# A three-stage fp32 kernel: wider blocks at the end of its first MLP, and Pool's work cut into pieces

## The chip, the cores and the metric

The kernel runs on one core of one Trainium2 chip, in one launch. The metric is device time in microseconds (us). The core has a matrix engine (PE, with its weight loads shown apart as PEld), a vector engine (DVE), a scalar engine (ACT), GpSimd (called POOL in the profile, Pool here) and a queue (SP) that issues the DMA transfers. Each engine works through its own list of instructions in the order in which they were written down; engines wait for each other by semaphores.

## The reference

Three stages, all in fp32, each fed by the one before:

```python
# attention: q, k, v are (4, 8, 576, 64); everything below max - tau is masked
scores = q @ k.T / sqrt(64)
scores = where(scores >= max(scores) - tau, scores, -1e9)
x = softmax(scores) @ v                  # then (2304 tokens, 512)
# first MLP: 512 -> 2048 -> 512
h = x @ w_in;  y = (h / (1 + exp(-h))) @ w_out
# second MLP: 512 -> 1536 -> 512
out = ((y @ w_a) * (y @ w_b)) @ w_o2
```

## The kernel before, in words

**Products.** A product in fp32 is made of passes in a faster format: each operand is cut into a high and a low part (`hi`, `lo` in the code: hi is a rounded copy made by ACT, lo is the difference) and three passes are summed in PSUM (weights low, weights high, other operand low). A pass loads 128x128 weights and streams the other operand's columns: 256 columns in the first MLP (`TB = 256`, nine blocks of tokens), 512 in the second (`T2 = 512`).

**Weights.** They come from HBM as pairs of 32-bit words. One chunk (128x512) goes through `split_weight`: ACT copies the low word (L314), ACT or DVE scales the high one (L319/L321, tile `wc`, one buffer), DVE takes its sign (L325, in place in `wraw`) and joins both (L330), Pool adds the words (`total`, L334, tile `wt`), ACT rounds (`hi`, L338), and Pool or DVE subtracts (`lo`, L342). The first MLP has 32 chunks, prepared during attention, all with `lo` on Pool; the second has 36, alternately on Pool and DVE.

**Attention.** A tile is 128 queries by 576 keys. PE makes the scores (L483, later L476), DVE scales them and takes the minimum (L492), adds tau (`thr`, L498 in the first 16 tiles, L500 behind them), ACT takes the exponential (L504/L506), DVE masks and sums (L509), PE transposes (L541; L539 are filler transposes), ACT copies out of PSUM (L548), PE multiplies by v (L586). Pool divides by the sums (L621) and, in the later heads, makes a low part of q (L407; k's on DVE, L404). The result x goes to DRAM.

**First MLP.** Block j of 256 tokens: x is read back and cut (`xr`; hi on ACT L676, lo on Pool L679). For each of 16 slices f of the hidden size: 12 passes up (L704, PSUM bank `hb` or `hc`), tanh on ACT (L713), gate on DVE (L716), hi on ACT (L719), lo on DVE (L722), 12 passes down (L754, PSUM pair `sb` or `sd`). The passes of later blocks lie between attention's.

**Second MLP.** Up passes L833 into `ps_a` and `ps_b`, L840 to L849 for the product and its parts, down passes L877.

**What sets the order.** Every operation is a task of a `Plan` with an engine, a cost in ns, a rank and the tasks it needs. `Plan.run` plays them through with these costs and writes each engine's list in the order of its play. Tasks marked `port` are DVE's that use the SBUF port that DVE has together with Pool; the plan makes such a task, and any Pool task, longer by what the other has still to run, at most by its own cost (`SHARED = 1.0`). `closed` is the point where attention's buffers are given back and those of the later stages opened; `closed1` is the same behind the first MLP.

Of the kernel before, what the change touches and what calls it, by code (L numbers as in the profile page):

```python
# [21 lines left out]
P = 128  # L22
# [10 lines left out]
NB = NT // TB  # L33
# [25 lines left out]

SCALE_ON = ("ACT",)  # L60


class Plan:
# [15 lines left out]

    SHARED = 1.0  # L80
# [42 lines left out]
    def run(self):  # L123
# [17 lines left out]
        while events:  # L141
# [13 lines left out]
            for e, q in ready.items():  # L155
                if idle[e] and q:
# [50 lines left out]
def fused_kernel(ctx: ExitStack, tc: tile.TileContext, qk, qk2, v, tau, w_in, w_out, w_a, w_b, w_o2, out):  # L207
# [19 lines left out]
    def pool(stack, name, bufs, side="left", **kw):  # L227
# [22 lines left out]
    ps_1 = pool(p1, "ps_1", 1, space=PSUM)  # L250
    ap = {n: pool(att, n, RINGS[n]) for n in ("qk", "v", "t", "e", "pa", "pb")}
# [36 lines left out]

    def dma(rank, nbytes, fn, n=1, **kw):

        return pl.add("SP", 400 * n, rank, fn, nbytes=nbytes, **kw)
# [8 lines left out]
    def split_weight(key, src, rank, dst, after=(), lo_engine="Pool", scale_engine="DVE"):  # L300
# [32 lines left out]
        def total():  # L333
            nc.gpsimd.tensor_tensor(out=s["t"], in0=s["c"].bitcast(U32), in1=s["t"], op=ALU.add)  # L334
# [5 lines left out]
        def lo():  # L340
            eng = nc.gpsimd if lo_engine == "Pool" else nc.vector
            eng.tensor_tensor(out=wt[key][:, 1, :], in0=s["t"].bitcast(F32), in1=wt[key][:, 0, :].bitcast(F32),  # L342
                              op=ALU.subtract)
# [10 lines left out]
        i = pl.add("ACT", act_ns(512), rank, hi, [t], [dst], behind=after)  # L354
        o = pl.add(lo_engine, pool_ns(512) if lo_engine == "Pool" else dve_ns(512), rank, lo, [i], port=True)
        pl.free("wt", o)
        w_ready[key] = (i, o)
        return [a, l, c, h, j, t, i, o]
# [33 lines left out]
    def split_head(n, b, h):  # L392
# [13 lines left out]
        def lo_q():  # L406
            nc.gpsimd.tensor_tensor(out=s["t"][D:, 0], in0=s["r"][D:, :S], in1=s["t"][D:, 0].bitcast(F32), op=ALU.subtract)  # L407
# [3 lines left out]
        q = add("Pool", pool_ns(S), n + R_SPLIT, lo_q, [up])  # L411
        k = add("DVE", dve_ns(S), n + R_SPLIT, lo_k, [up], port=True)
        att_tasks.append(ld)
        pl.free("qk", q, k)
        s["ready"] = [q, k]
# [42 lines left out]
    def softmax(parts, total):  # L458
# [10 lines left out]
        def scores():  # L469
            s["s"] = (ps_1 if bank == "sb" else ps_s).tile([P, 2, 512], F32, name=bank)  # L470
# [24 lines left out]
        def threshold():  # L495
            s["thr"] = sm_p.tile([P, 1], F32, name="thr")
            if early:
                nc.vector.tensor_scalar(out=s["thr"], in0=s["min"], scalar1=back, scalar2=tsub, op0=ALU.mult, op1=ALU.add)  # L498
            else:
                nc.vector.tensor_add(out=s["thr"], in0=s["min"], in1=tadd)  # L500
# [27 lines left out]
    def weigh(b, half, c, tiles, v, last):  # L528
# [91 lines left out]
        def divide():  # L620
            nc.gpsimd.tensor_tensor(out=s["x"][:, :nq], in0=s["x"][:, :nq], in1=s["i"][:, :nq], op=ALU.mult)  # L621
# [9 lines left out]
        dv = add("Pool", pool_ns(nq), last_n + R_EV, divide, [ld])  # L631
        pl.free("xi", dv)
        st2 = dma(-1, P * 4 * nq, store, after=[dv])
        pl.free("x", st2)
        att_tasks.extend([st, ld, st2])
# [54 lines left out]
    def mlp1_up(n, j, f):  # L690
# [34 lines left out]
        for c in range(NC):  # L725
            p = pl.add("PE", 3 * pe_ns(TB), R, up(c),
# [4 lines left out]
            if f == NF - 1:  # L731
                pl.free("xb", p)
        th = pl.add("ACT", act_ns(TB, True), R_AUX, tanh, [p], ["g", "th"])
        ga = pl.add("DVE", dve_ns(TB), R_AUX, gate, [th])
        pl.free(bank, ga)
        hh = pl.add("ACT", act_ns(TB), R_AUX, hi, [ga])
        ll = pl.add("DVE", dve_ns(TB), R_AUX, lo, [hh], port=True)
        pl.free("th", ll)
        g_ready[j, f] = (hh, ll)

    def mlp1_down(n, j, f):


        ring = "sd" if j * NF >= TWO_H and j % 2 == 0 else "sb"
        prods = [(e, a, "gh") for e in range(NC) for a in (1, 0)] + [(e, 0, "gl") for e in range(NC)]

        def down(k0):
            def fn():
                if f == 0 and k0 == 0:
                    ys[j] = (pools["hc"] if ring == "sd" else ps_1).tile([P, 2, 512], F32, name=ring).rearrange("p k (e t) -> p (k e) t", e=2)  # L750
                w = wt["out", f]
                for e, a, g in prods[k0:k0 + 4]:

                    nc.tensor.matmul(ys[j][:, e, :], lhsT=w[:, a, e * P:(e + 1) * P], rhs=gs[j, f][g],  # L754
                                     start=(f == 0 and e % 2 == 0 and a == 1), stop=(f == NF - 1 and g == "gl"),
# [4 lines left out]
        for k0 in (0, 4, 8):  # L760
            p = pl.add("PE", 4 * pe_ns(TB), R, down(k0), [g_ready[j, f][k0 == 8], *w_ready["out", f]],
                       [ring] if f == 0 and k0 == 0 else [], behind=[down_last[0]])
            down_last[0] = p
        w_last["out", f] = p
        pl.free("g", p)
        if f == NF - 1:
            def halve(k):
                def fn():
                    ys[j, k] = yo_p.tile([P, 2, TB], F32, name="yo")
                    if k == 0:  # L770
                        nc.scalar.activation(out=ys[j, k], in_=ys[j][:, 2 * k:2 * k + 2], func=AF.Copy, scale=0.5)
                    else:
                        nc.vector.tensor_scalar(out=ys[j, k], in0=ys[j][:, 2 * k:2 * k + 2], scalar1=0.5, scalar2=None, op0=ALU.mult)
# [232 lines left out]
```

## Time and profile before

| | |
|---|---|
| runs | 1191.71 us, median of 3 (1190.04 to 1193.56) |
| profiled execution | 1190.77 us; its span in the trace 1189.0 us |
| PE busy | 1154.5 us (97%), 7675 passes |
| PE weight loads busy | 994.4 us (84%) |
| DVE busy | 646.2 us (54%) |
| ACT busy | 543.9 us (46%) |
| POOL busy | 255.2 us (21%) |
| granted TensorE clock | 1.00 of full speed (2.4 GHz) |

Shares over the whole span hide the stages. The page cuts the span into 40 slices of 29.7 us; a digit is the busy share of a slice in tenths. PE shows 7, 8 and 9 in the first seven slices and 9 nearly everywhere behind them; DVE shows 7 to 9 in the first seven, then 7 and 8 while attention lasts (to slice 16), little in the rest of the first MLP, 5 to 7 in four or five slices round its end, and 1 to 3 behind them; POOL is busy in the first seven slices and round the end of the first MLP. PE's ends are modelled, so its busy time says little between 95 and 100%; the times from start to start of its passes say more.

### The profile page before, as it was taken

Reading aid. Unit: us, or ns where it says so; the run is one execution under the profiler, and the core shown is the slowest. Engines: PE = TensorE matmul, PEld = TensorE weight load, DVE = VectorE, ACT = ScalarE, POOL = GpSimd, SP = SyncE. Lnnn points to the kernel's source line nnn. Section 1 sums busy time; section 2 is a strip of 40 time slices with the busy share of each in tenths; the row PEclk is TensorE's granted clock in tenths of the full one; section 3 lists DMA queues with packets and bytes.
Section 4 is the critical chain, followed back from the end, with each engine's and each line's share of the span. In section 5 each row is a group of like instructions: output and inputs, shape, how many; then the busy total and the mean of one; then the engine's idle time right before and its main releaser. Section 6 shows DMA issues by size and latency. Waiting matters only on the chain.

```text
span 1189.0 us, 19705 instructions
## 1 busy us (share of the span) xinstructions
PE 1154.5 (97%) x7675; PEld 994.4 (84%) x7675; DVE 646.2 (54%) x1448; ACT 543.9 (46%) x1071; POOL 255.2 (21%) x212
## 2 busy tenths in 40 slices
PE   8879999999999999989999999999999999999998
PEld 6556667898898888989999999877888888888898
DVE  7989897777777877473233257775211311211121
ACT  7777786666666766553233245443211211211121
POOL 3655554222111311131000034553000000000000
PEclk9999999999999999999999999999999999999999
DMA  5654543222322320261010024441100200000010
GB/s 192 197 175 144 168 155 132 77 85 81 100 74 71 108 73 33 67 191 54 1 37 28 1 72 143 127 139 56 69 1 1 71 1 1 18 36 1 1 36 18
DMA packets 43277, 90.15 MB, mean 76 GB/s; under 512 B 4384, under 2 KB 22448, under 8 KB 43184
## 3 DMA queue, kind: packets, MB, share of 16 engines
q1 hardware_dynamic: 43040, 88.89, 23.5%
q8 instruction: 60, 0.98, 0.3%
q14 instruction: 33, 0.27, 0.1%
q10 hardware_dynamic: 144, 0.00, 0.0%
HBM read 74.65 MB, written 14.23 MB: 75 GB/s over the span
## 4 chain that ended last, share of the span: by engine, by line
PE 65%; DVE 5%; DMA 3%; POOL 2%; issue 2%; ACT 1%; SPq 0%; POOLq 0%; DVEq 0%; ACTq 0%
PE op L877 11%; PE ps_b L833 11%; PE ps_a L833 10%; PE hb L704 8%; PE sb L754 7%; PE sd L754 4%; PE hc L704 4%; PE av L586 3%; PE sa L476 3%; PE tp L541 3%; POOL wt L334 2%; DVE wc L330 1%; DMA wraw<-w_a 1%; DVE wraw L325 1%; DVE wc L321 1%
## 5 line engine op out<-in xcount | busy, mean ns | idle before, releaser
L704 PE MATMUL hb<-xh,w 128*128 128x256 f32 x832 | 164.3, 291 | 3.1 <-DVE th L716 1.4
L843 DVE TENSOR_TENSOR z<-ps_b,z 128x512 f32<-128x512 f32 (+1 forms) x60 | 38.2, 637 | 230.8 <-PE ps_b L833 230.8
L833 PE MATMUL ps_a<-yh,w 128*128 128x512 f32 (+1 forms) x480 | 137.1, 370 | 0.3 <-POOL w L342 0.3
L833 PE MATMUL ps_b<-yh,w 128*128 128x512 f32 (+1 forms) x480 | 136.7, 369 | 0.4 <-DVE w L342 0.4
L704 PEld LDWEIGHTS hb<-xh,w 128*128 128x128 f32 x832 | 128.9, 191 | 9.1 <-issue 4.3
L877 PE MATMUL op<-w,zh 128*128 128x512 f32 x432 | 134.3, 392 | 0.0
L492 DVE TENSOR_SCALAR_CACHE_REDUCE t<-sa,nscale 128x576 f32<-128x576 f32 x128 | 103.5, 808 | 48.9 <-PE sa L476 47.6
L509 DVE SCALAR_TENSOR_TENSOR e<-t,thr,e 128x576 f32<-128x576 f32 x128 | 114.1, 891 | 16.7 <-ACT e L506 15.3
L704 PE MATMUL hb<-xl,w 128*128 128x256 f32 x416 | 117.5, 283 | 0.0
L334 POOL TENSOR_TENSOR wt<-wc,wt 128x512 uint32<-128x512 uint32 x68 | 91.9, 1351 | 114.2 <-DVE wc L330 93.4
L754 PE MATMUL sb<-gh,w 128*128 128x256 f32 x768 | 115.9, 286 | 0.0
L541 PE MATMUL tp<-ident,e 128*128 128x128 f32 x706 | 104.7, 277 | 10.6 <-DVE e L509 7.4
L506 ACT ACTIVATE e<-t,min 128x576 f32<-128x576 f32 x128 | 99.8, 782 | 25.4 <-DVE t L492 24.7
L840 ACT COPY z<-ps_a 128x512 f32<-128x512 f32 (+1 forms) x60 | 32.6, 543 | 163.1 <-PE ps_a L833 163.1
L541 PEld LDWEIGHTS tp<-ident,e 128*128 128x128 f32 x706 | 78.8, 140 | 32.4 <-DVE e L509 12.3
L754 PEld LDWEIGHTS sb<-gh,w 128*128 128x128 f32 x768 | 101.1, 191 | 3.3 <-issue 2.8
L833 PEld LDWEIGHTS ps_a<-yh,w 128*128 128x128 f32 x480 | 87.4, 188 | 17.3 <-POOL w L342 0.7
L833 PEld LDWEIGHTS ps_b<-yh,w 128*128 128x128 f32 x480 | 86.7, 188 | 16.2 <-DVE w L342 0.9
L877 PEld LDWEIGHTS op<-w,zh 128*128 128x128 f32 x432 | 80.3, 188 | 16.9
L846 ACT CAST zh<-z 128x512 fp32r<-128x512 f32 (+1 forms) x60 | 34.6, 577 | 128.3 <-DVE z L843 128.3
L722 DVE TENSOR_TENSOR gl<-th,gh 128x256 fp32r<-128x256 f32 x144 | 72.7, 505 | 33.9 <-ACT gh L719 33.6
L833 PE MATMUL ps_a<-yl,w 128*128 128x512 f32 (+1 forms) x240 | 88.9, 370 | 0.0
(97 smaller groups left out, 2173.3 us busy)
## 6 DMA issues: line engine op xcount, KB each, us to landing
qk<-qk SPq DMA_DIRECT2D x20, 576.0 KB
wraw<-w_in SPq DMA_DIRECT2D x16, 512.0 KB
wraw<-w_out SPq DMA_DIRECT2D x16, 512.0 KB
v<-v SPq DMA_DIRECT2D x20, 320.0 KB
wraw<-w_a SPq DMA_DIRECT2D x12, 512.0 KB
wraw<-w_b SPq DMA_DIRECT2D x12, 512.0 KB
wraw<-w_o SPq DMA_DIRECT2D x12, 512.0 KB
xr<-xT_d SPq DMA_DIRECT2D x36, 128.0 KB
```

Source lines behind the costliest of these rows:

```text
L334: nc.gpsimd.tensor_tensor(out=s["t"], in0=s["c"].bitcast(U32), in1=s["t"], op=ALU.add)
L476: nc.tensor.matmul(s["s"][:r + m, j, :NH], lhsT=hd["t"][:, 0, c - r:c + m], rhs=hd["t"][:, k, j * NH:(j + 1) * NH], start=(k == 1), stop=( ...
L492: nc.vector.tensor_scalar(out=s["t"], in0=s["s"][:, :, :NH], scalar1=nscale, scalar2=None, op0=ALU.mult, op1=ALU.min, accum_out=s["min"])
L506: nc.scalar.activation(out=s["e"], in_=s["t"], func=AF.Exp, scale=-1.0, bias=s["min"])
L509: nc.vector.scalar_tensor_tensor(out=s["e"], in0=s["s"][:, :, :NH] if early else s["t"], scalar=s["thr"], in1=s["e"], op0=ALU.is_ge if ear ...
L541: nc.tensor.transpose(t["tp"][:, j * P:(j + 1) * P], e["e"][:, o:o + P], ident)
L704: nc.tensor.matmul(s["h"], lhsT=w[:, a, o:o + P], rhs=xx, start=(c == 0 and k == 0), stop=(c == NC - 1 and k == 2))
L722: nc.vector.tensor_sub(out=s["gl"], in0=s["t"], in1=s["gh"].bitcast(F32))
L754: nc.tensor.matmul(ys[j][:, e, :], lhsT=w[:, a, e * P:(e + 1) * P], rhs=gs[j, f][g], start=(f == 0 and e % 2 == 0 and a == 1), stop=(f == ...
L833: nc.tensor.matmul(s[nm][:, :tn], lhsT=w[:, a, o:o + P], rhs=yy[:, :tn], start=(c == 0 and k == 0), stop=(c == NC - 1 and k == 2))
L843: nc.vector.tensor_mul(out=s["z"][:, :tn], in0=s["b"][:, :tn], in1=s["z"][:, :tn])
L877: nc.tensor.matmul(o_ps[t0, i], lhsT=s[z][:, i * P:(i + 1) * P], rhs=wt["o2", f][:, a, :], start=(f == 0 and k == 0), stop=(f == NF2 - 1 a ...
```

## The change

Two blocks of 512 tokens stand at the end of the first MLP in place of four of 256. They have buffers of their own (pool `b5`, open from `closed` on), an own PSUM bank for each of their output parts (`yc`, `yd`, `ye`, `yf`, or `sb`), and their loads of x stand behind `closed`. In the weights of the first MLP, `lo` moves from Pool to DVE. Pool's operations outside the second MLP's weights are cut into pieces of at most 128 columns. In attention's `thr`, L500 becomes a `tensor_scalar` with one per-partition operand where it was a `tensor_add`, and L498 takes a constant in place of one of its two. The plan lengthens a shared task by all that the other engine has still to run. The buffers of the second MLP's input are split in two (four for even blocks, four behind `closed1` for odd ones), its first four weight chunks go to the ring `w`, which comes free in the last block of the first MLP, and its last four to `w2`, which now opens at `closed1`.

```diff
-NB = NT // TB
+BLOCKS = tuple((i * TB, TB) for i in range(5)) + ((5 * TB, 512), (5 * TB + 512, 512))
+PIECE = 128
+LO_ON = ("DVE",)
...
-                        shared = max(0, min(port["Pool" if e == "DVE" else "DVE"] - now, t["cost"]))
-                        port[e] = end = done = end + self.SHARED * shared
+                        port[e] = end = done = end + max(0, port["Pool" if e == "DVE" else "DVE"] - now)
...
+def pieces(n, most):
+    k = -(-n // most)
+    return [slice(n * i // k, n * (i + 1) // k) for i in range(k)]
...
+    def on_pool(n, rank, fn, after, most):
+        ts = []
+        for o in pieces(n, most):
+            ts.append(pl.add("Pool", pool_ns(o.stop - o.start), rank, lambda o=o: fn(o), after, behind=ts[-1:]))
+        return ts
...
-        t = pl.add("Pool", pool_ns(512), rank, total, [j, l])
-        pl.free("wc", t)
+        ts = on_pool(512, rank, total, [j, l], most)
+        pl.free("wc", ts[-1])
...
-        engines = dict(scale_engine=SCALE_ON[i % len(SCALE_ON)])
+        engines = dict(scale_engine=SCALE_ON[i % len(SCALE_ON)], lo_engine=LO_ON[i % len(LO_ON)], most=PIECE)
...
-                nc.vector.tensor_add(out=s["thr"], in0=s["min"], in1=tadd)
+                nc.vector.tensor_scalar(out=s["thr"], in0=s["min"], scalar1=tadd, scalar2=None, op0=ALU.add)
...
-            ld = dma(-1, P * 4 * TB, load, after=need, take=["xr"], slack=SLACK)
-            h = pl.add("ACT", act_ns(TB), R_AUX, hi, [ld], ["xb"])
-            l = pl.add("Pool", pool_ns(TB), R_AUX, lo, [h])
-            pl.free("xr", l)
+            ld = dma(-1, P * 4 * tn, load, after=need, take=[raw], slack=SLACK, behind=[closed] if big else [])
+            h = pl.add("ACT", act_ns(tn), R_AUX, hi, [ld], [ring])
+            l = on_pool(tn, R_AUX, lo, [h], PIECE)[-1]
+            pl.free(raw, l)
...
-        ring = "sd" if j * NF >= TWO_H and j % 2 == 0 else "sb"
+        banks = {4: ("yc", "yd"), 5: ("ye", "yf", "sb"), 6: ("yc", "yd", "ye", "yf")}.get(j, ("sb",))
+        per = T2 // tn
...
-        split_weight(key, src, 1e6 + i, "w2" if i < RINGS["w2"] else "w", [closed], ("Pool", "DVE")[i % 2])
+        split_weight(key, src, 1e6 + i, *(("w", [closed]) if i < 32 else ("w2", [closed1])), ("Pool", "DVE")[i % 2])
```

How the lists change is read from the built programs. First DVE in the tiles behind the sixteenth, before the change; `t` and `e` are a tile's scores and exponentials, `wraw` and `wc` a weight chunk:

```order
L492 TENSOR_SCALAR t,min<-sa,nscale 128x576
L500 TENSOR_TENSOR thr<-min,tadd 128x1
L492 TENSOR_SCALAR t,min<-sa,nscale 128x576
L509 SCALAR_TENSOR_TENSOR e,sum<-t,thr,e 128x576
L325 TENSOR_SCALAR wraw<-wraw 128x512
L500 TENSOR_TENSOR thr<-min,tadd 128x1
L330 SCALAR_TENSOR_TENSOR wc<-wc,wraw 128x512
```

The same place now (L511, L519, L528 are the lines of scores, `thr` and mask; L341 and L346 of sign and join; L358 of `lo`):

```order
L358 TENSOR_TENSOR w<-wt,w 128x512
L341 TENSOR_SCALAR wraw<-wraw 128x512
L511 TENSOR_SCALAR t,min<-sa,nscale 128x576
L346 SCALAR_TENSOR_TENSOR wc<-wc,wraw 128x512
L519 TENSOR_SCALAR thr<-min,tadd 128x1
L528 SCALAR_TENSOR_TENSOR e,sum<-t,thr,e 128x576
```

Each chunk brings one more instruction on DVE, `lo` (L358), right ahead of the next chunk's sign. Pool in the same stretch, before:

```order
L342 TENSOR_TENSOR w<-wt,w 128x512
L334 TENSOR_TENSOR wt<-wc,wt 128x512
L621 TENSOR_TENSOR x<-x,xi 128x256
```

And now (L350 is `total`, L640 the division, L702 the low part of x):

```order
L350 TENSOR_TENSOR wt<-wc,wt 128x128 x4
L702 TENSOR_TENSOR xl<-xr,xh 128x128 x2
L350 TENSOR_TENSOR wt<-wc,wt 128x128 x7
L640 TENSOR_TENSOR x<-x,xi 128x128 x2
```

`lo` is gone from Pool, and each `total` stands there as four pieces. Last, PE in a late block of the first MLP, before (the end of one unit's up passes, a unit's down passes, the start of the next; a unit is a block's slice f):

```order
L704 MATMUL hc_9526<-xh_8542,w_2135 128x256 x2
L704 MATMUL hc_9526<-xl_8543,w_2135 128x256
L754 MATMUL sd_9070<-gh_9510,w_2198 128x256 x8
L754 MATMUL sd_9070<-gl_9511,w_2198 128x256 x4
L704 MATMUL hb_9563<-xh_8455,w_1926 128x256 x2
L704 MATMUL hb_9563<-xl_8456,w_1926 128x256
```

And now, where the first block of 512 (`ye`, `yf`, `sb`) ends and the last (x parts from 7292 on) begins; L730 are the up passes and L790 the down passes:

```order
L790 MATMUL sb_7664<-gl5_8087,w_2535 128x512 x2
L730 MATMUL hb_8148<-xh5_7292,w_247 128x512 x2
L730 MATMUL hb_8148<-xl5_7293,w_247 128x512
L730 MATMUL hb_8148<-xh5_8107,w_329 128x512 x2
L730 MATMUL hb_8148<-xl5_8108,w_329 128x512
L730 MATMUL hb_8148<-xh5_8113,w_388 128x512 x2
L730 MATMUL hb_8148<-xl5_8114,w_388 128x512
L790 MATMUL ye_7662<-gh5_8128,w_2645 128x512 x2
L790 MATMUL yf_7663<-gh5_8128,w_2645 128x512 x2
L790 MATMUL sb_7664<-gh5_8128,w_2645 128x512 x4
```

A unit keeps its 12 passes up and 12 down, each now over 512 columns, so the four former blocks' 4 x 16 x 24 passes become 2 x 16 x 24. At the seam, the last unit's down passes of the first wide block stand between the third and the fourth part of x of the second.

## Rows read from the trace of the kernel before

**Rows 1.** Busy time by stage: stretch, length, engine busy (instructions), PEclk, DMA share, GB/s.
```profile
0.00:210.00 210.00, 186.26 (x1330) 133.33 (x1331) 184.64 (x423) 159.34 (x304) 110.28 (x93) 1.00 0.52 165
...
210.00:490.00 280.00, 277.78 (x2257) 249.68 (x2257) 212.16 (x580) 184.96 (x359) 58.85 (x48) 1.00 0.24 76
...
490.00:545.00 55.00, 51.34 (x413) 48.90 (x410) 32.87 (x63) 24.09 (x55) 14.58 (x13) 1.00 0.46 141
...
690.00:840.00 150.00, 148.95 (x831) 129.46 (x830) 100.67 (x166) 68.19 (x125) 62.77 (x46) 1.00 0.36 113
```

**Rows 2.** The chain that ended last, merged: start us, us, engine, what, count.
```profile
554.70 1.44 PE sb L754 x12
...
850.85 2.75 PE ps_a L833 x12
```

**Rows 3.** Timeline, 600 us: start us, us, engine line op out<-in xcount [idle before].
```profile
600.62 1.12 PE L754 MATMUL sd<-gh,w 128*128 128x256 f32 x8
...
600.82 0.38 ACT L713 ACTIVATE th<-hc 128x256 f32<-128x256 f32 x1 [0.51 <-PE hc L704]
...
601.69 0.41 ACT L719 CAST gh<-th 128x256 fp32r<-128x256 f32 x1 [0.49 <-DVE th L716]
...
603.50 0.76 PE L754 MATMUL sd<-gh,w 128*128 128x256 f32 x5
```

**Rows 4.** DVE by line, 0-210 us: xcount, busy us, mean ns, idle before.
```profile
L509 DVE SCALAR_TENSOR_TENSOR e<-t,thr,e 128x576 f32<-128x576 f32 x41 | 40.4, 985 | 4.3 <-ACT e L506 4.0
...
L325 DVE TENSOR_SCALAR wraw<-wraw 128x512 uint32<-128x512 uint32 x32 | 29.9, 935 | 3.7 <-ACT wc L319 3.0 <-DMA xi<-r_d 0.4
...
L500 DVE TENSOR_TENSOR thr<-min,tadd 128x1 f32<-128x1 f32 x41 | 15.0, 366 | 0.4
...
L722 DVE TENSOR_TENSOR gl<-th,gh 128x256 fp32r<-128x256 f32 x18 | 10.7, 596 | 0.7 <-ACT gh L719 0.6
```

**Rows 5.** Single lines: ns minimum/median/maximum, first and last start us, shapes.
```profile
L325 DVE TENSOR_SCALAR wraw<-wraw x32: 414/1028/1517, 10.2 to 182.0; 128x512 uint32<-128x512 uint32 x32
...
L498 DVE TENSOR_SCALAR thr<-min,back,tsub x16: 259/272/277, 8.1 to 49.2; 128x1 f32<-128x1 f32 x16
...
L334 POOL TENSOR_TENSOR wt<-wc,wt x32: 1263/1279/1792, 11.6 to 184.9; 128x512 uint32<-128x512 uint32 x32
```

**Rows 6.** Timeline round 100 us: DVE and POOL.
```profile
101.33 0.15 DVE L500 TENSOR_TENSOR thr<-min,tadd 128x1 f32<-128x1 f32 x1
...
101.51 1.30 POOL L342 TENSOR_TENSOR w<-wt,w 128x512 fp32r<-128x512 f32 x1 [0.73 <-ACT w L338]
...
102.04 1.07 DVE L325 TENSOR_SCALAR wraw<-wraw 128x512 uint32<-128x512 uint32 x1 [0.56 <-ACT wc L319]
...
103.96 0.80 DVE L509 SCALAR_TENSOR_TENSOR e<-t,thr,e 128x576 f32<-128x576 f32 x1
...
104.11 1.79 POOL L334 TENSOR_TENSOR wt<-wc,wt 128x512 uint32<-128x512 uint32 x1 [1.30 <-DVE wc L330]
...
104.70 1.48 DVE L722 TENSOR_TENSOR gl<-th,gh 128x256 fp32r<-128x256 f32 x1
```

**Rows 7.** Windows, L342 alone: DVE busy (count), POOL busy (count).
```profile
690.00:840.00 150.00, 11.67 (x16) 22.45 (x16) 1.00 0.36 113
```

**Rows 8.** DVE and POOL by line, 545 to 690 us.
```profile
L722 DVE TENSOR_TENSOR gl<-th,gh 128x256 fp32r<-128x256 f32 x50 | 21.2, 425 | 23.6 <-ACT gh L719 23.6
...
L679 POOL TENSOR_TENSOR xl<-xr,xh 128x256 fp32r<-128x256 f32 x12 | 8.8, 740 | 102.7 <-PE hc L704 51.8 <-ACT xh L676 50.8
```

**Rows 9.** PE waits, 0 to 210 us: us in total, times, longest.
```profile
PE tp L541 <- DVE e L509: 7.4, 16, 1.5
...
PE sa L483 <- DVE t L492: 4.9, 7, 1.6
```

**Rows 10.** The same, 490 to 545 us.
```profile
PE sd L754 <- ACT gh L719: 2.8, 4, 1.7
...
PE sd L754 <- DVE gl L722: 0.9, 2, 0.7
```

More of the change, by code (lines that the diff above doesn't have):

```diff
@@ L298, in fused_kernel, with split_weight @@
     wt, w_ready = {}, {}
-    def split_weight(key, src, rank, dst, after=(), lo_engine="Pool", scale_engine="DVE"):
+    def split_weight(key, src, rank, dst, after=(), lo_engine="Pool", scale_engine="DVE", most=512):
         s = {}
@@ L350, in split_weight @@
         j = pl.add("DVE", dve_ns(512), rank, join, [h, c], port=True)
-        t = pl.add("Pool", pool_ns(512), rank, total, [j, l])
-        pl.free("wc", t)
+        ts = on_pool(512, rank, total, [j, l], most)
+        pl.free("wc", ts[-1])
         pl.free("wraw", j, l)
[L354 to L358, printed above, removed]
+        i = pl.add("ACT", act_ns(512), rank, hi, [ts[-1]], [dst], behind=after)
+        if lo_engine == "Pool":
+            os = on_pool(512, rank, lo, [i], most)
+        else:
+            os = [pl.add("DVE", dve_ns(512), rank, lambda: lo(slice(0, 512)), [i], port=True)]
+        pl.free("wt", os[-1])
+        w_ready[key] = (i, os[-1])
+        return [a, l, c, h, j, *ts, i, *os]
     def w1_chunk(i, rank):
         j, i = divmod(i, 8)
-        engines = dict(scale_engine=SCALE_ON[i % len(SCALE_ON)])
+        engines = dict(scale_engine=SCALE_ON[i % len(SCALE_ON)], lo_engine=LO_ON[i % len(LO_ON)], most=PIECE)
         if i < 4:
@@ L760, in mlp1_down @@
         for k0 in (0, 4, 8):
-            p = pl.add("PE", 4 * pe_ns(TB), R, down(k0), [g_ready[j, f][k0 == 8], *w_ready["out", f]],
-                       [ring] if f == 0 and k0 == 0 else [], behind=[down_last[0]])
+            p = pl.add("PE", 4 * pe_ns(tn), R, down(k0), [g_ready[j, f][k0 == 8], *w_ready["out", f]],
+                       banks if f == 0 and k0 == 0 else [], behind=[down_last[0], *([closed] if j >= 4 and f == 0 else [])])
             down_last[0] = p
         w_last["out", f] = p
-        pl.free("g", p)
+        pl.free("g5" if big else "g", p)
@@ L780, in mlp1_down @@
             evs = []
-            for k in range(2):
-                ev = pl.add(("ACT", "DVE")[k], (act_ns, dve_ns)[k](2 * TB), -2, halve(k), [p], ["yo"])
+            for k in range(NC // per):
+                ev = pl.add(("ACT", "DVE")[k % 2], (act_ns, dve_ns)[k % 2](T2), -2, halve(k), [p], [outs[k]])
                 evs.append(ev)
-                st = dma(-1, 2 * P * 4 * TB, store(k), after=[ev])
-                pl.free("yo", st)
-                y_dma.append(st)
-            pl.free(ring, *evs)
+                st = dma(-1, P * 4 * T2, store(k), after=[ev])
+                pl.free(outs[k], st)
+                y_dma.append((t0, tn, st))
@@ L790, in fused_kernel @@
+            for i, bk in enumerate(banks):
+                pl.free(bk, *(evs[i:] if bk == "sb" else evs[i:i + 1]))
+            if j == 5:
+                b_done.extend(evs[2:])
     y2, y2_ready, zs, z_ready, o_ps = {}, {}, {}, {}, {}
@@ L793, in load_y @@
         tn = min(T2, NT - t0)
-        need = y_dma[2 * (t0 // TB):2 * ((t0 + tn) // TB)]
+        need = [t for a, m, t in y_dma if a < t0 + tn and a + m > t0]
+        ab = "ab"[t0 // T2 % 2]
         def split(c):
@@ L919, in close_attention, with close_b @@
         open_transit()
[L920 to L921 removed]
+        pools["ya"] = pool(ctx, "ya", 4, "right")
+        pools["b5"] = pool(p1, "b5", 1)
         pools["hc"] = pool(p1, "ps_hc", 1, space=PSUM)
+        pools["y5"] = pool(p1, "ps_y5", 1, space=PSUM)
+    def close_b():
+        psb.close()
         pools["ab", 0] = pool(ctx, "ps_ab", 1, "right", space=PSUM)
     closed = pl.add("none", 1, 0, close_attention, behind=[*att_tasks, *closed0])
[L926 removed]
+    units = [(j, f) for j in range(len(BLOCKS)) for f in range(NF)]
     for n, u in enumerate(units):
@@ L945, in close_mlp1 @@
         pools["ab", 1] = pool(ctx, "ps_ab2", 1, space=PSUM)
-    closed1 = pl.add("none", 1, 0, close_mlp1, behind=[up_last[0], down_last[0], closed, *y_dma])
+        pools["w2"] = pool(ctx, "wpool2", RINGS["w2"])
+        pools["yb"] = pool(ctx, "ybb", 4)
+    closed_b = pl.add("none", 1, 0, close_b, behind=[closed, *b_done])
+    closed1 = pl.add("none", 1, 0, close_mlp1, behind=[up_last[0], down_last[0], closed, closed_b, *(t for *_, t in y_dma)])
     for i in range(36):
```

133 lines of the change are left out of this document (74 added, 59 removed).

## The prediction

> **What bounds the kernel now.** I read the windows by stage first, because shares of the whole span mix stages [rows 1]. From 210 us on PE is the bound: it is busy 277.78 of 280 us, and 148.95 of 150 us round the end of the first MLP, at a granted clock of 1.00 (the 2.4 GHz level) throughout. There only fewer or cheaper passes help. Two stretches are different. From 0 to 210 us PE is busy 186.26 us, so 23.7 us are open, and DVE is nearly as busy (184.64). From 490 to 545 us PE has 51.34 of 55.
>
> Then the waits of PE in the first stretch: transposes waiting for the mask's result 7.4 us and scores' buffers waiting for DVE's scaling 4.9 us, together 12.3 of the 23.7 [rows 9]. So about half of a microsecond of DVE's that comes or goes there reaches PE. In the second stretch PE waits for ACT's gh 2.8 us and DVE's gl 0.9 us [rows 10].
>
> Last DVE's groups and single lines, because DVE's time there is partly waiting. The sign takes 935 ns in the mean and 414 at best [rows 4, 5]. The threshold, one column, takes 366 in the mean [rows 4], yet 0.15 us where it runs undisturbed [rows 6]. The timeline shows what they wait for: Pool's `lo` runs from 101.51 to 102.81, and the sign that starts at 102.04 ends at 103.11, 0.30 behind Pool's end [rows 6]. So such an instruction of DVE waits until Pool's current one is over, and is then served. In the other direction Pool's `total` starts at 104.11, beside a mask that ends at 104.76, and takes 1.79 in place of its usual 1.28 [rows 5, 6]; the gl that starts at 104.70 ends at 106.18, just behind Pool.
>
> **The change part by part. First, the width.** Four blocks of 256 with 16 units of 24 passes are 1536 passes; they become 768 of 512 columns. Twelve passes of 256 take 1.44 us, 120 ns each, and twelve of 512 take 2.75 us, 229 ns each [rows 2]. So 184.3 us become 176.0: -8.3 us, all of it in the PE-bound part. With both rows' rounding and a few ns more or less on either width, -7.0 to -9.6.
>
> The Trainium skill ("TensorE: Matmul & The Clock Gate", section Back-to-back issue gap) gives 262 and 518 cycles for 256 and 512 columns at full clock. An estimate by this page is 768 x 2.5 ns = 1.9 us of gain in place of 8.3. The trace differs from it, with 240 ns against 229 for the same columns.
>
> What hides the handover from up to down must still hide it. A block's unit ends its up passes at 600.82, gh is there at 602.10, and the down passes that read it start at 603.50, because another unit's passes stand between [rows 3]. At 512 ACT's and DVE's links double to about 2.6 us, and the passes between double too: cost nothing. If that cover were missing, each of 32 units would lose up to 2.6 us; the order keeps the distance, so I leave that out.
>
> **DVE in the first stretch.** What goes: 32 signs no longer meet Pool's `lo`, 32 x (0.935 - 0.414) = -16.7 us. The threshold changes its form, and the nearest row of a form with per-partition scalars, L498, takes 259 to 277 ns all 16 times while Pool works beside it [rows 5]: it never waits. So the waits of 41 thresholds go, 41 x (0.366 - 0.15) = -8.9. Mask and gl carry 41 x (0.985 - 0.80) = 7.6 and 18 x (0.596 - 0.425) = 3.1 of waits [rows 4, 6, 8], and part of them is behind `total`, which stays on Pool in pieces; I take half, -5.4. What comes: 32 `lo` on DVE at 11.67/16 = 0.73 [rows 7], +23.4; and the new threshold's own length, which no row shows, between 0.15 (L500) and 0.27 (L498), say 0.21, +2.5. Net -5.1 us.
>
> The pieces have no row. Pool takes 740 ns for 256 columns and 1279 for 512 [rows 5, 8], so 2.1 ns a column and 0.2 fixed, and a piece of 128 is about 0.47 us, four of them 1.88. A wait behind one piece is then 0.47 at most, where it was up to 1.28. But one `total` has four pieces, and DVE may meet more than one. If every `total` costs DVE two meetings of a full 0.47, 32 x 2 x 0.47 = +30 us stand against the 5.3 of waits that I left; with a threshold of 0.27 besides, the net is about +22. If nothing waits any more, it is -5.1 - 5.3 = -10. With a share of half, PE gets -3 us (-6 to +11); a little over half of 5.1, since DVE is the longer of the two there.
>
> The Trainium skill ("SBUF — State Buffer", section Who interferes with whom) says that the shared pair is held for a whole instruction, and counts `tensor_scalar` without accumulator among the operations that can take it. By that page the new threshold would still wait, and some 3 us of the 8.9 would come back on DVE, 1.5 on PE. The row of L498, with its 18 ns between smallest and largest, speaks against it.
>
> **The rest.** In the seam from 490 to 545 us fewer chunks and no `lo` of Pool's stand in DVE's and Pool's way at attention's end; of the 3.7 us that PE has open I take 1.5 back (-3.5 to +2). From 210 to 490 us PE is full: 0 (-2 to +2). The second wide block's x is cut by Pool in 4 x 4 pieces, 7.5 us, beside the first wide block's 88 us (16 x 24 x 0.229); its buffers come free one after another, and the order puts a unit's down passes between the third and fourth part, so PE covers most: +0.5 (0 to +5, where the four parts are cut only after the first block's last up passes). The loads of x wait for `closed`: SP has nothing urgent behind them, and DMA is at a share of 0.46 or less behind 210 us [rows 1], so 0. The second MLP's first four weight chunks now take buffers that come free in the last block; that block is 88 us long where it was 46 (16 x 24 x 0.120), so chunks have longer: -0.2, at most the 1.05 us that PE has open there now [rows 1].
>
> **The sum** against the profiled execution's 1190.77: -8.3 - 3 - 1.5 + 0.5 - 0.2 = -12.5, which gives 1178.3. The runs' median is 0.9 higher, so 1179 us.
>
> **Rivals.** (a) *Pieces multiply the waits.* Pool's lists hold four instructions where there was one, and whenever DVE has several such operations in a row, a piece can slip in between each pair. For it: the mask and the join are long and come close together, and `lo` adds a fifth operation of that kind per chunk. Against: the trace shows DVE served as soon as Pool's current instruction is over, and Pool's time in `total` grows only from 1.28 to 1.88 per chunk while its `lo` goes, 22.45/16 = 1.40 each [rows 7]. Price: DVE's net +22, reaching PE by half to whole, +11 to +22; with -8.3 and -1.5 that is 1192 to 1203 us. It turns the change into a loss when the DVE net is over about +10 (whole) or +20 (half).
>
> (b) *The front stage gets all of it.* DVE's net is -10 and most reaches PE, the seam gives back 3.5: -8.3 - 9 - 3.5 = -21, or about 1170. For it: DVE's queue is what PE's largest waits name. Against: half of PE's open time in that stretch names other things.
>
> (c) *Width saves nothing.* If all of the 120 ns grows with the columns, a wide pass costs 240 in this block, and the first term is 0: 1187. By the page on TensorE above it would be 1185. Against: the 512-wide rows of the same trace, 229.
>
> (d) *The second wide block starts late.* The four parts are cut behind the first block's end, +5 in place of +0.5: 1184. Against: the order places all the loads far ahead.
>
> **Numbers.** My forecast, with its own range 1174 to 1184, gets 0.53; (b) 0.16; (d) 0.07; (c) 0.04, as no change; (a) 0.20, half of it near no change and half slower. A measurement of this kernel tells about 0.3% (3.6 us) from no change, so faster means under 1188: 0.53 + 0.16 + 0.07 = 0.76; same 0.04 + 0.10 = 0.14; slower 0.10. The range is 1167 to 1192: below (b) by its own uncertainty, and up to the mild end of (a).
>
> **What would show it.** Right: 24 passes of a wide unit take 5.5 us and the stretch of the wide blocks holds no PE wait; the sign's mean falls from 935 towards 450 ns and the threshold's minimum and maximum lie within 50 ns; DVE's busy time up to 210 us falls by about 5 us, and the point where attention ends comes 3 to 5 us earlier. Wrong: signs, masks or joins keep means 200 ns or more over their best times (rival a); 24 passes take 5.7 us (c); PE has a gap of some us at the second wide block's first unit (d). The forecast fails most easily in the share of DVE's saving that reaches PE, since the plan also reorders this stage.

## The result and the profile after

The changed kernel takes 1173.14 us (median of 4, 1172.42 to 1174.95) against 1191.57 (median of 4) before, a ratio of 0.9843 (95% interval 0.983 to 0.9856): 18.4 us faster, where 12.5 were forecast. It lies in the stated range, and 1 us below the likeliest case's own. The profiled executions differ by less, 1190.77 to 1174.95, or 15.8 us (spans 1189.0 and 1173.2).

Start times of PE's passes cut a span into three: A, from the span's first busy instruction to the first pass of the block that is the first wide one now (the sixth block's, before); B, from there to the second MLP's first pass; C, from there to the end of the last pass.

| us | A | B | C |
|---|---|---|---|
| before | 550.0 | 184.9 | 450.1 |
| changed | 547.9 | 175.0 | 446.2 |
| difference | -2.1 | -9.9 | -3.9 |

Busy time by stage (the columns of [rows 1]):

```profile
0.00:210.00 210.00, 186.23 (x1316) 133.53 (x1317) 171.38 (x448) 155.89 (x299) 92.39 (x191) 0.98 0.52 164
...
210.00:490.00 280.00, 279.13 (x2271) 250.81 (x2270) 207.34 (x584) 187.07 (x363) 89.34 (x160) 1.00 0.23 75
...
490.00:545.00 55.00, 53.27 (x442) 52.87 (x441) 25.39 (x51) 20.96 (x50) 14.48 (x25) 1.00 0.36 112
...
545.00:690.00 145.00, 145.00 (x660) 120.89 (x659) 59.27 (x87) 47.82 (x81) 22.30 (x25) 1.00 0.13 42
```

DVE has 13.3 us less to do up to 210 us, but PE's busy time there is what it was, 186.23 against 186.26, and its clock is 0.98. So PE's open time up to 210 us is 23.8 us, where it was 23.7: what DVE gained stands as idle time. Only behind 210 us is PE's open time shorter, 0.9 us against 2.2 up to 490, and 1.7 against 3.7 from there to 545. Attention's last product starts at 486.9 us, 4.8 us earlier than before (491.7), but the first MLP's passes between it and the wide blocks then take 2.7 us more. DVE's groups up to 210 us answer to [rows 4], with `lo` (L358) new:

```profile
L528 DVE SCALAR_TENSOR_TENSOR e<-t,thr,e 128x576 f32<-128x576 f32 x40 | 35.6, 891 | 11.6 <-ACT e L525 10.4
...
L358 DVE TENSOR_TENSOR w<-wt,w 128x512 fp32r<-128x512 f32 x32 | 22.7, 709 | 4.2 <-ACT w L354 3.4
...
L341 DVE TENSOR_SCALAR wraw<-wraw 128x512 uint32<-128x512 uint32 x32 | 13.8, 431 | 0.6 <-ACT wc L335 0.6
...
L749 DVE TENSOR_TENSOR gl<-th,gh 128x256 fp32r<-128x256 f32 x18 | 8.7, 484 | 3.2 <-ACT gh L746 3.2
...
L519 DVE TENSOR_SCALAR thr<-min,tadd 128x1 f32<-128x1 f32 x40 | 8.3, 207 | 0.4
```

The sign's mean is down from 935 to 431 ns, the mask's from 985 to 891, the threshold's from 366 to 207. But the mask's idle time ahead, waiting for ACT's exponential, has gone from 4.3 to 11.6 us. The threshold by itself (minimum, median, maximum in ns):

```profile
L519 DVE TENSOR_SCALAR thr<-min,tadd x40: 174/208/217, 51.4 to 208.8; 128x1 f32<-128x1 f32 x40
```

PE's waits up to 210 us, against [rows 9], and from 490 to 545 us, against [rows 10]:

```profile
PE tp L560 <- DVE e L528: 8.3, 11, 2.2
...
PE sa L502 <- DVE t L511: 4.5, 6, 1.6
```

```profile
PE yc L790 <- ACT gh L746: 1.2, 1, 1.2
...
PE yc L790 <- DVE gl L749: 0.6, 1, 0.6
```

The first two are where they were (12.8 us together, 12.3 before); the second two are down from 3.7 to 1.8 us. Where the granted clock falls in the first stretch, in windows of 5 us (PE busy, PEclk, DMA share, GB/s; PEclk is a window's mean over the two levels, 1.2 GHz counted as 0.5 and 2.4 GHz as 1):

```profile
65.00:70.00 5.00, 2.65 (x15) 0.91 0.47 150
...
70.00:75.00 5.00, 5.00 (x31) 0.75 0.39 140
...
180.00:185.00 5.00, 3.21 (x15) 0.68 0.44 138
...
185.00:190.00 5.00, 5.00 (x43) 0.98 0.32 116
```

Weighed by length, these windows miss 5 x (0.09 + 0.25 + 0.32 + 0.02) = 3.4 us of full clock. The profiled execution of before shows 1.00 throughout [rows 1]; in the executions of it that were timed later beside the experiments the mean clock was mostly 0.996 to 0.998 of the whole run, 2 to 5 us. The pair of profiles shows the change 2.6 us smaller than the medians do; that the clock is the reason is not shown (the fastest of the changed kernel's four executions, 1172.42 us, has the lowest mean clock, 0.994). What the engine did before the second fall, by the timeline:

```profile
180.16 0.66 ACT L330 ACTIVATE wt<-wraw 128x512 uint32<-128x512 uint32 x1 [2.30 <-DMA wraw<-w_out]
...
180.72 0.39 ACT L746 CAST gh<-th 128x256 fp32r<-128x256 f32 x1
...
181.15 0.50 DVE L749 TENSOR_TENSOR gl<-th,gh 128x256 fp32r<-128x256 f32 x1 [2.52 <-ACT gh L746]
...
181.57 0.17 DVE L460 RECIPROCAL sums<-sum 128x4 f32<-128x4 f32 x1
...
181.79 0.48 PE L610 MATMUL av<-ident,sums 128*128 128x128 f32 x1 [2.19 <-DVE sums L460]
```

ACT's copy of a weight chunk waits for its DMA; gh stands behind it in ACT's list, gl behind gh, the reciprocal behind gl in DVE's list, and PE waits 2.19 us for that. The 5 us from 180 have a clock of 0.68. What missed clock costs in this stretch cannot be read from its length. e3 below, with the same order, was profiled at a clock of 0.95 up to 210 us, 10.2 us of full clock missed:

```profile
0.00:210.00 210.00, 189.34 (x1305) 137.96 (x1306) 171.87 (x443) 155.12 (x298) 92.70 (x191) 0.95 0.53 162
```

Its A is still 0.6 us shorter than the changed kernel's. PE's open time there is 20.7 us against 23.8: the slower passes stand where PE would have waited.

Groups of twelve passes on the chain that ended last (start, us, engine, what, count), one of the first wide block, one of an even block of the second MLP and one of an odd block:

```profile
563.41 2.72 PE hc L730 x12
...
735.27 2.77 PE op L920 x12
...
826.28 2.72 PE op L920 x12
```

Against [rows 2] the wide passes of the first MLP and those of the second MLP's odd blocks take 2.72 (227 ns each), those of even blocks still 2.75 to 2.77. Before, PE also waited for weights in the second MLP's first units, which it no longer does; PE's waits before, 690 to 840 us:

```profile
PE ps_b L833 <- DVE w L342: 0.4, 1, 0.4
...
PE ps_a L833 <- POOL w L342: 0.3, 1, 0.3
```

### The profile page after: what moved, and what is told of

It is laid out like the page before. It is cut to its first block, busy times and chain, and to the rows that moved or that the text cites. A ratio compares the mean times of both kernels' runs of the same rounds, so it can differ in the third digit from the quotient of the medians.

```text
span 1173.2 us, 18253 instructions
## 1 busy us (share of the span) xinstructions
PE 1142.9 (97%) x6917; PEld 957.8 (82%) x6917; DVE 621.7 (53%) x1416; ACT 531.1 (45%) x999; POOL 271.4 (23%) x440
## 3 DMA queue, kind: packets, MB, share of 16 engines
q1 hardware_dynamic: 40864, 88.89, 23.7%
## 4 chain that ended last, share of the span: by engine, by line
PE 60%; DMA 2%; DVE 1%; ACT 1%; issue 0%; POOL 0%; SPq 0%; ACTq 0%; POOLq 0%
PE ps_a L876 13%; PE op L920 13%; PE ps_b L876 13%; PE hb L730 5%; PE hc L730 4%; PE sb L790 3%; PE yc L790 2%; PE yd L790 1%; PE ye L790 1%; PE yf L790 1%; DMA wraw<-w_a 1%; PE av L605 1%; PE tp L560 1%; PE sa L495 1%; DMA wraw<-w_b 1%
## 5 line engine op out<-in xcount | busy, mean ns | idle before, releaser
L730 PE MATMUL hb<-xh,w 128*128 128x256 f32 (+1 forms) x704 | 155.2, 310 | 1.5 <-DVE th L743 1.0
L350 POOL TENSOR_TENSOR wt<-wc,wt 128x128 uint32<-128x128 uint32 (+1 forms) x164 | 111.2, 702 | 140.2 <-DVE wc L346 98.7
L511 DVE TENSOR_SCALAR_CACHE_REDUCE t<-sa,nscale 128x576 f32<-128x576 f32 x128 | 103.7, 810 | 50.6 <-PE sa L495 45.6
L528 DVE SCALAR_TENSOR_TENSOR e<-t,thr,e 128x576 f32<-128x576 f32 x128 | 111.5, 871 | 26.4 <-ACT e L525 24.8
L730 PEld LDWEIGHTS hb<-xh,w 128*128 128x128 f32 x704 | 113.0, 190 | 10.9 <-issue 2.3
L730 PE MATMUL hb<-xl,w 128*128 128x256 f32 (+1 forms) x352 | 106.5, 303 | 0.7 <-POOL xl L702 0.7
L790 PE MATMUL sb<-gh,w 128*128 128x256 f32 (+1 forms) x576 | 97.6, 300 | 0.0
L790 PEld LDWEIGHTS sb<-gh,w 128*128 128x128 f32 x576 | 80.0, 190 | 5.9 <-issue 3.3
L920 PE MATMUL op<-w,zl 128*128 128x512 f32 x216 | 84.6, 392 | 0.0
L749 DVE TENSOR_TENSOR gl<-th,gh 128x256 fp32r<-128x256 f32 (+1 forms) x112 | 63.9, 571 | 28.3 <-ACT gh L746 28.1
L876 PE MATMUL ps_a<-yha,w 128*128 128x512 f32 (+1 forms) x288 | 77.4, 355 | 0.0
L876 PE MATMUL ps_b<-yha,w 128*128 128x512 f32 (+1 forms) x288 | 77.0, 354 | 0.0
L640 POOL TENSOR_TENSOR x<-x,xi 128x128 f32<-128x128 f32 (+2 forms) x80 | 40.9, 535 | 147.1 <-issue 49.9
L702 POOL TENSOR_TENSOR xl<-xr,xh 128x128 fp32r<-128x128 f32 x72 | 37.0, 542 | 161.0 <-ACT xh L699 156.4
```

Source lines behind the costliest of these rows:

```text
L350: nc.gpsimd.tensor_tensor(out=s["t"][:, o], in0=s["c"][:, o].bitcast(U32), in1=s["t"][:, o], op=ALU.add)
L511: nc.vector.tensor_scalar(out=s["t"], in0=s["s"][:, :, :NH], scalar1=nscale, scalar2=None, op0=ALU.mult, op1=ALU.min, accum_out=s["min"])
L528: nc.vector.scalar_tensor_tensor(out=s["e"], in0=s["s"][:, :, :NH] if early else s["t"], scalar=s["thr"], in1=s["e"], op0=ALU.is_ge if ear ...
L640: nc.gpsimd.tensor_tensor(out=s["x"][:, o], in0=s["x"][:, o], in1=s["i"][:, o], op=ALU.mult)
L730: nc.tensor.matmul(s["h"], lhsT=w[:, a, o:o + P], rhs=xx, start=(c == 0 and k == 0), stop=(c == NC - 1 and k == 2))
L749: nc.vector.tensor_sub(out=s["gl"], in0=s["t"], in1=s["gh"].bitcast(F32))
```

## The experiments

Times are medians; each ratio is to the kernel before, run beside it on the same chip (the changed kernel's is 0.9843). In e1, e2, e3, e6, e7, e8 and e12 every engine keeps the changed kernel's order but for the edit; in e4, e5, e9, e11 and e13 the plan was made anew.

| run | us | ratio (95%) | A | B | C |
|---|---|---|---|---|---|
| e4_wide_only | 1185.53 | 0.9935 (0.9916-0.9954) | 555.4 | 180.8 | 445.2 |
| e5_narrow | 1208.25 | 1.0134 (1.0113-1.0155) | 547.0 | 184.8 | 470.0 |
| e9_narrow_w2 | 1192.60 | 1.0002 (0.999-1.0013) | 547.4 | 184.8 | 453.2 |
| e1_whole | 1183.93 | 0.9928 (0.991-0.9946) | 559.6 | 174.8 | 446.2 |
| e7_whole_total | 1175.43 | 0.9862 (0.984-0.9884) | 552.5 | 174.8 | 446.2 |
| e8_halves | 1175.58 | 0.9874 (0.985-0.9898) | 547.5 | 176.1 | 446.2 |
| e2_lo_pool | 1181.35 | 0.9918 (0.9893-0.9942) | 554.0 | 175.1 | 446.2 |
| e13_pool_planned | 1184.13 | 0.9932 (0.9914-0.995) | 558.0 | 174.8 | 446.2 |
| e3_thr_add | 1174.58 | 0.9858 (0.9836-0.9881) | 547.3 | 175.0 | 446.2 |
| e6_fill | 1176.25 | 0.987 (0.985-0.989) | 548.8 | 175.1 | 446.2 |
| e11_slack | 1176.16 | 0.9864 (0.9846-0.9882) | 549.5 | 175.6 | 445.2 |
| e12_align | 1173.59 | 0.9842 (0.9822-0.9861) | 550.5 | 175.3 | 443.9 |

A, B and C are those of one profiled execution each. A carries most of the clock's falls, and the mean clocks of one kernel's executions differ by some 3 us. B and C hold only small waits, but for e4's B and for C in e5 and e9. e7's profiled execution is its slowest (1179.36 us, the others 1175.2 to 1176.2), so its A is too long for its median. In e7 only `total` is whole; in e8 the pieces run in pairs, 256 columns each.

**The width alone.**

```diff
-PIECE = 128
+PIECE = 512
...
-LO_ON = ("DVE",)
+LO_ON = ("Pool",)
...
-nc.vector.tensor_scalar(out=s["thr"], in0=s["min"], scalar1=tadd, scalar2=None, op0=ALU.add)
+nc.vector.tensor_add(out=s["thr"], in0=s["min"], in1=tadd)
```

(L517's form and the plan's rule for shared tasks are the old ones too.)

> Width and the second MLP's buffers alone: the first weights' lo is on Pool again, Pool's operations are whole, both thresholds have their old forms and the plan its old rule. Theory 1 (all of the gain is width and what follows it; the DVE part of the change gives PE nothing): stretch up to 210 us as before, 768 wide passes at 227 ns save 9.8 us, the second MLP 3.4 us, the seam behind attention 0 to 2: 1176 to 1179 us. Theory 2 (the cheaper DVE reaches PE by half and brought the rest): 1181 to 1184 us, and the waits of gh and gl behind attention are there as before (some 4 to 5 us).

1185.5 is above both theories' ranges, and neither's account holds. C is shorter, as theory 1 had it, and PE's waits behind attention are 3.8 us as before, as theory 2 had it (in e9 below they are 0.3: the shorter seam comes with the rest of the change). But A is 5.4 us longer than before although its operations are those of before, and B holds 5.8 us more than the changed kernel's. There PE waits behind ACT (3.9 us in the rows, three times), by the timeline:

```profile
730.99 0.67 ACT L330 ACTIVATE wt<-wraw 128x512 uint32<-128x512 uint32 x1 [1.66 <-DMA wraw<-w_b]
...
732.90 0.62 ACT L746 CAST gh<-th 128x512 fp32r<-128x512 f32 x1 [0.76 <-DVE th L743]
...
733.57 0.73 PE L790 MATMUL yc<-gh,w 128*128 128x512 f32 x2 [1.92 <-ACT gh L746]
```

The head of ACT's list waits 1.66 us for a weight chunk of the second MLP; gh comes late and PE stands 1.92.

**All but the width.**

```diff
-BLOCKS = ... + ((5 * TB, 512), (5 * TB + 512, 512))
+BLOCKS = ... + tuple((i * TB, TB) for i in range(5, 9))
```

> The changed kernel with nine blocks of 256 again (the weights, the pieces, the thresholds and the second MLP's buffers stay as changed). Theory 1: 9.8 us are lost and the second MLP keeps its 3.4: 1182 to 1184 us. Theory 2 says about 1180 to 1182 for the same kernel (8.3 us for the width by the second MLP's passes). If the second MLP's gain comes with the long last block, it is gone too: 1186 us, with waits of some 1.3 us at the second MLP's weights.

> Nine blocks of 256 as in the earlier run, but the second MLP's first four weight chunks have buffers of their own again, open from attention's end as in the kernel before. If the 23 us that the second MLP lost in the earlier run came from these chunks having to wait for buffers that come free in a last block of only 46 us, the second MLP takes 445 to 448 us again and the whole 1184 to 1188. If they came from something else in nine narrow blocks (x, the input's buffers), it stays near 1208. The stretch of the last four blocks takes 185 to 186 us, against 175.2 for the two wide ones.

(In both the PSUM banks of the narrow blocks follow.) B is 184.8 in both, as before, so the two wide blocks are worth 9.8 to 9.9 us. e5's C of 470.0 refutes the first two cases, and the third had the waits at 1.3 us. PE's largest wait from 690 to 840 us in e5, and in e9, where four chunks have buffers of their own:

```profile
PE ps_a L876 <- POOL w L358: 15.0, 3, 6.2
```

```profile
PE ps_a L876 <- POOL w L358: 2.9, 1, 2.9
```

Behind these waits the granted clock falls too: it is 0.93 from 690 to 840 us in e5, and 0.93 from 805 to 830 us in e9. The new buffers of the second weights thus need the long last block. With the old ones, all but the width comes to 1.0002: A gets 2.6 us shorter, C is 3.1 longer than before. The 1184 expected of e9 was wrong for its C, 7.0 us longer than the changed kernel's. That wait is 2.9 us of it and the missed clock behind it at most 1.8; the rest was not traced.

**The pieces, at a fixed order.**

```diff
-rank, lambda o=o: fn(o), after, behind=ts[-1:]
+rank, (lambda: None) if ts else (lambda: fn(slice(0, n))), after, behind=ts[-1:]
```

> Every group of Pool's pieces runs as one whole operation at the place of its first piece; the order on all engines stays. Theory 1 (DVE no longer binds the first stretch): DVE is 3 to 5 us busier up to 210 us by waits, and the time stays within 2 us of the changed kernel: 1172 to 1175 us. Theory 2 (half of DVE's time reaches PE): 1175 to 1177. Rival that the pieces cost more than they save: Pool's total takes 1.28 in place of 1.69 and weights are ready sooner, 1170 to 1172.

> Only the weights' total is whole on Pool; q's low part, x's division and x's low part stay in pieces; the order stays. The kernel with all of them whole lost 6.7 us up to 220 us and 4.7 us more from there to 480 us. If totals make the first loss and q's low parts and the divisions the second: 1177 to 1180 us, with no further loss behind 220 us. If the totals do not matter, 1173 to 1175; if they make all of it, 1183.

> Pool's pieces are run in pairs (256 columns in place of 128) at the places of the first of each pair; the order stays. If the time follows the longest wait behind one Pool instruction, it lies between the pieces of 128 (1173 us) and the whole operations (1184): 1175 to 1179. If any cut will do, 1173; if only short pieces help, 1181 to 1184.

Whole operations cost 10 to 11 us, all in A: theory 1 (DVE no longer binds, 1172 to 1175) falls, and theory 2's half (1175 to 1177) is far too small as well. Whole totals alone cost 2.3 us by the medians, and the intervals of the ratios overlap; the 4.6 in A is that of their slowest execution. Halves cost nothing that can be told from the pieces of 128. The rest of e1's loss needs the other operations; which of them was not tested one by one. PE's open time from 210 to 490 us is 3.1 us in e1 against 0.9:

```profile
210.00:490.00 280.00, 276.90 (x2225) 246.58 (x2225) 215.04 (x586) 186.31 (x357) 61.26 (x48) 1.00 0.26 81
```

A candidate is q's low part, 576 columns long. DVE's own low part of k, in the same stretch, changed kernel and then e1:

```profile
L423 DVE TENSOR_TENSOR sp<-qk,sp 128x576 fp32r<-128x576 f32 x18 | 15.6, 868 | 2.2 <-ACT sp L420 2.1
```

```profile
L424 DVE TENSOR_TENSOR sp<-qk,sp 128x576 fp32r<-128x576 f32 x19 | 24.9, 1311 | 2.5 <-ACT sp L421 2.5
```

It takes 0.44 us more, 18 times.

**`lo` on Pool.**

```diff
-eng = nc.gpsimd if lo_engine == "Pool" else nc.vector
+eng = nc.gpsimd if lo_engine == "Pool" or most < 512 else nc.vector
```

> The first weights' lo is run by Pool, whole, at the places of DVE's; all else keeps its order. Theory 1: DVE loses 22.7 us of lo up to 210 us and gets 10 to 16 us of waits in sign, mask and join; Pool gets 44 us; the time changes little or is worse, since Pool's chain of weights is longer: 1173 to 1177 us. Theory 2 (DVE's busy time is what counts, by half): 1169 to 1172 us.

> The changed kernel with the first weights' lo back on Pool, in pieces of 128 like Pool's other operations, and the plan made anew for it (the earlier run had lo on Pool at the places planned for DVE, and lost 8 us). Width alone gave 1185.5 us, all of the change 1173. If the move of lo to DVE is what the first stretch needs, this comes near the kernel with the width alone: 1181 to 1186 us, with signs, masks and joins waiting for Pool some 10 to 20 us up to 210 us. If the short pieces are enough and lo may stay on Pool once the order is made for it: 1173 to 1177, with the sign's mean below 0.6 us.

e2 (whole, at the planned places) loses 8 to 9 us against the changed kernel, more than either theory allowed, and e13 (`LO_ON = ("Pool",)`, pieces, planned anew) loses 11, as its first case had it. In e2 the sign waits again:

```profile
L341 DVE TENSOR_SCALAR wraw<-wraw 128x512 uint32<-128x512 uint32 x32 | 31.8, 994 | 13.5 <-ACT wc L335 13.5
```

In e13 it does not much (558 ns), and DVE is busy only 155 us; there Pool is the long one, 164 of 210 us:

```profile
0.00:210.00 210.00, 186.29 (x1297) 133.75 (x1297) 155.36 (x400) 152.11 (x292) 164.32 (x312) 0.96 0.53 158
```

```profile
184.46 2.14 POOL L358 TENSOR_TENSOR w<-wt,w 128x128 fp32r<-128x128 f32 x4
...
186.63 0.67 ACT L330 ACTIVATE wt<-wraw 128x512 uint32<-128x512 uint32 x1 [3.12 <-POOL w L358]
...
189.50 0.63 DVE L341 TENSOR_SCALAR wraw<-wraw 128x512 uint32<-128x512 uint32 x1 [4.45 <-ACT wc L335]
...
190.51 0.80 PE L730 MATMUL hb<-xh,w 128*128 128x256 f32 x2 [4.48 <-DVE th L743]
```

Pool's `lo` in four pieces takes 2.14 us, ACT waits 3.12 us for it, the sign 4.45 for ACT, and PE 4.48 for a gate (`th`) that stands behind the sign in DVE's list. Over the whole stretch PE is as busy as in the changed kernel (186.29 us against 186.23), with 1297 passes against 1316 and a clock of 0.96 against 0.98. So `lo` on Pool loses here, whole or in pieces, and the waits above lead to Pool's chain.

**Smaller parts.** e3 puts `tensor_add` back; e6 adds 18 filler transposes at two waits of PE; e11 adds `slack=1500` to each weight's load; e12 adds a tile of 64 bytes ahead of the even input buffers.

> Only the threshold of the later tiles has its old form again (tensor_add); the order on all engines stays. The threshold then waits for Pool again: in the first stretch its mean goes from 0.21 to 0.3 or more with pieces of 0.4 us, some 3 to 6 us of DVE. If half of DVE's time there reaches PE: 1175 to 1177 us. If a wait of one column's work is hidden (ACT's exponential runs at the same time): 1172 to 1174. If Pool's current piece is short enough, the mean is below 0.21 in the calm stretches and the time falls to 1171.

The threshold's mean goes from 207 to 263 ns:

```profile
L519 DVE TENSOR_TENSOR thr<-min,tadd 128x1 f32<-128x1 f32 x39 | 10.2, 263 | 0.4
```

That is 2 us of DVE, and no time that can be told.

> The changed kernel with 18 more filler transposes in each of two places where PE waits for DVE and its granted clock then falls (ahead of the transposes that start at 67.2 us, and ahead of the sums' transpose at 181.8 us). If the lower clock behind these two waits is what eats DVE's saving in the first stretch, the granted clock stays 1.00 there and the time falls by 2 to 3.5 us, to 1170 to 1171. If the clock does not depend on these waits, or falls elsewhere instead, it stays at 1173 to 1174; if the fillers stand in the way, 1174 to 1176.

No gain. The clock stays up behind the second wait (180 to 185 us) and falls ahead of it, and earlier in the stretch:

```profile
50.00:55.00 5.00, 3.56 (x21) 0.74 0.57 184
...
60.00:65.00 5.00, 3.56 (x18) 0.77 0.75 231
...
175.00:180.00 5.00, 4.38 (x22) 0.66 0.60 131
...
180.00:185.00 5.00, 5.00 (x47) 1.00 0.36 109
```

> The plan counts 1.5 us more for the landing of each weight chunk, so ACT's first copy of a chunk stands later in its list; the plan is made anew. If PE's remaining waits in the first stretch come from ACT standing behind a weight's DMA (8.1 us of such waits up to 210 us, one of them 2.3 us ahead of the longest wait of PE), ACT's waits for weights fall below 4 us and the time to 1168 to 1171. If PE's waits come from the chains of the scores themselves, 1172 to 1175; a new order by itself moves the first stretch by 2 to 5 us either way, as the kernel with only the width showed.

ACT's waits for w_out's chunks rose from 4.5 to 6.9 us, and the time by some 2 to 3, with intervals that overlap. Whether those waits bind the first stretch stays open.

> The changed kernel with 64 bytes of gap ahead of the second MLP's even input buffers, so that they begin at the same place within 512 bytes as the weights and the odd blocks' buffers. Same instructions and order on all engines. In the changed kernel a pass of 512 takes 226.7 ns in the odd blocks and 229 to 232 in the even ones. If the buffers' place decides this, the even blocks fall to 227 as well, and the second MLP takes 442.5 to 443 us in place of 444.4: 1171 to 1172 us. If it is something else about even blocks, nothing changes: 1173 to 1174.

C falls by 2.3 us, as the place of the buffers would have it; an even block's group of twelve:

```profile
778.87 2.72 PE op L920 x12
```

A was 2.6 us longer in the profiled execution, at a mean clock of 0.992, and the median is the same as the changed kernel's. It is the best version of C, but not shown to be faster as a whole.

## Why the forecast was right, and where its terms were off

- **Width: -8.3 forecast, -9.9 measured (B).** The mechanism is shown: 12 passes in 2.72, a unit's 24 in 5.44, no wait at the block seam (0 where I had +0.5) and the handover hidden. The size failed because I took the 2.75 of the second MLP for a wide pass, 2 ns a pass too much; e12 shows, for the changed kernel's even blocks, that the place of the buffers makes such a difference. An estimate by the table of the Trainium skill ("TensorE: Matmul & The Clock Gate", Back-to-back issue gap) was 1.9 us; the runs disagree with it, 9.9.
- **DVE in the first stretch: net -5.1, half of it to PE.** Both halves of this step were off. The net was larger: DVE's busy time fell by 13.3 us, of which signs -16.1, thresholds -6.7, `lo` +22.7, masks -4.8, gl -2.0 and sums -2.7 (5.3 to 2.6), together -9.6 with one tile less in the stretch. These are near my lower bound of -10, since the pieces left little of the masks' waits. The Trainium skill ("SBUF — State Buffer", Who interferes with whom) counts the threshold's new form among those that can contend with GpSimd; at 174 to 217 ns in all 40 cases it shows no wait, and the 3 us that I put on one had no row behind them. But the share that reaches PE was not half: up to 210 us it was none (open time 23.7 and 23.8 us). PE's waits for DVE stayed, and DVE's idle time grew: the mask's wait for ACT's exponential alone from 4.0 to 10.4 us. The clock missed 3.4 us, at a cost that is open. The seam gave 1.9 us of PE's open time (1.5 forecast) and the stretch from 210 to 490 us 1.3 (0 forecast). Together A got 2.1 us shorter (2.6 in e9) where -3 and -1.5 were forecast. The clock, of which the trace of before showed no fall, was no term of mine.
- **The second MLP: -0.2 forecast, -3.9 measured (C).** I held the weights' edit for nearly free. It removes waits (0.7 us in the rows, 1.3 from start to start of passes), and the odd blocks' passes became 2 to 3 ns shorter, which I had not thought of.
- **The total was partly luck.** Against the sum, A fell 2.4 us short, B and C gave 2.1 and 3.7 us more (B with the block seam's +0.5), and the medians another 2.6 over the pair of profiles. One term too large took back part of two that were too small.
- **Rivals.** (a) did not happen: masks, joins and signs stand close to their best times. Its price was real on the other side: with whole operations or `lo` on Pool the same order is 8 to 11 us slower. (b) was near in time (1170) for another reason: the 13.3 us of DVE did not reach PE. (c) and (d) are refuted by B.
- **Left open.** The parts do not add: width alone (with the second MLP's new buffers) gave 7.5 us, all else (with the old ones) 0, both 18.4. What is shown of the rest: e4 loses 5.8 us in B to ACT's list and 7.5 in A, e9 7.0 in C. e4 loses 5.4 in A also against before, with the same operations. Its profile has 5.1 us of missed clock in A, where before has none, and 1.4 us more of PE's open time. In the same way missed clock is 8.5 us of A in e1 and e2 and 10.2 in e13, against the changed kernel's 3.4, so it could be 5 to 7 of the 12, 6 and 10 us by which their A is longer. But e3 misses 10.2 us and loses nothing, so how much of these losses is clock, and how much the waits ahead of its falls, stays open.

## What to carry to other kernels

Take a pass's price from a row with the same operands in the same place, not only the same shape. Time saved on one engine of a stage that waits counted here only up to the next engine's chain: look what that engine waits for next. And undoing one part in an order made for it prices that order, not the part: the part alone in the old kernel was worth nothing here.

## What the hardware showed beyond that

A pass of 512 took 226.7 ns in the wide blocks and in the second MLP's odd blocks. In its even blocks passes took 226 to 237 ns, 229 to 230 in the mean of the up passes. Moving only the even blocks' input buffers by 64 bytes brought those to 226.7 as well and took 2.3 us from C (e12). So the time of a pass can depend on where its moving operand begins; which places are good, and why, was not measured beyond these two. The passes of the down product, whose own operands stay where they were, got faster as well (a group of twelve from 2.77 to 2.72 us), so a pass's own operand is not the whole rule.

The two lengths together tell what width is worth: a pass of 256 takes 120.0 ns [rows 2] and one of 512 takes 226.7, both at a granted clock of 1.00. The 106.7 ns between them are 256 columns at one per period of 2.4 GHz (0.417 ns). What is left, some 13.3 ns, is the same in both: an estimate from these two rows of what each pass costs besides its columns. 768 passes fewer at 13.3 ns are 10.2 us, next to the 9.9 of B.
